# Seven common score banks, with the value sums of two units in any of them and added up by GpSimd

## The chip, the cores and the metric

The kernel uses one core of a Trainium2 chip. The metric is device time in microseconds, of one execution. TensorE (PE in the profile) multiplies and writes to PSUM, which has eight banks of 128 x 512 fp32; VectorE (DVE) and ScalarE (ACT) read PSUM; GpSimd (POOL) works on SBUF alone; the sync engine (SP) issues most DMAs.

## The reference

Two mixers of one input are gated and added. All is fp32; S = 2048 rows, D = 512 columns, 32 heads of 16.

```python
g = _sigmoid((x * gate_w).sum(-1, keepdims=True))
a = x @ dft_hid_re.T                     # hidden transform, real part
b = x @ dft_hid_im.T                     # and imaginary part
y_a = dft_seq_re @ a - dft_seq_im @ b    # 2048 x 2048 times 2048 x 512, twice
q, k, v = split(x @ wqkv)                # 32 heads of 16
p = softmax(q @ k.T * 16 ** -0.5)        # 2048 x 2048 for each head
y_b = concat(p @ v) @ wo
return g * y_a + (1 - g) * y_b
```

The softmax needs the maximum of each row of scores, or the exponentials overflow: the weights are scaled by 64.

## The kernel before

Products that need more than one fast fp32 pass are done in three: each operand is split into a high and a low part (`hi_lo`), and high x high, high x low and low x high are added in PSUM (`mm3`).

**Stages.** First q and k are made and stored, then v (into `vt`, 33 columns for each pair of heads: 16 of the even head, a column of ones, 16 of the odd head), then the imaginary hidden transform. Then comes the long middle part, which interleaves attention with the other work in three stages by one hand-written order: THIN (13 pairs of segments, beside the real hidden transform `real`), FULL (96 pairs, beside the sequence transform `dft`) and NINE (13 pairs, beside the output projection `proj`). An end part does the last pair of heads and what is left of the projection.

**Units.** Heads go in 16 pairs. The two heads of a pair lie in two halves of the partitions (`h` = 0, 1). For a pair and 1024 query columns, a unit `u` is one of 16 blocks of 128 keys: four score matmuls `s` (two blocks of 512 queries, two heads), each read by an exp on ACT into `pt` (four buffers), and then four value matmuls that take `pt` against 17 columns of `vt` (16 values and the ones, which give the sum of the row). The four go to four column groups of the array at the same time and add up over the 16 units in one PSUM bank, `acc`. After the 16th, ACT copies `acc` to `oe` and two DMAs store it.

**Maxima.** Well ahead of that, `a` tiles compute the same scores the other way round (128 queries by 512 keys), and DVE reduces each to its row maxima (`mx`). When all tiles of a pair and half are reduced, `m_parts` (DVE, then two small GpSimd operations) and, a segment later, `m_rows` (a DVE transpose, then four DMAs on SP's queue and four on GpSimd's) put the negative maxima as two extra rows under q, so that the score matmul subtracts them.

**A segment.** A pattern string is a segment; a letter is a slot. In each slot a matmul `d` of the interleaved work runs in one half of the rows (64 of 128), and a score, `a` or `s`, in the other half at the same time. Two letters in a slot are two scores and no `d`. `|` is the value matmuls of one unit, which use all rows. A pair of segments does the same `d`s with the one half of the rows and then with the other. The first `d` of a segment is given a wait by hand: for a reader of a score of the last slot of the segment before (`before`, `users`).

**Banks.** Scores `s` have a pool of three banks (`psS`), `a` tiles three (`psA`), `acc` one and `d` one (`psD`). A matmul into a bank waits until its last content has been read. Engines take their instructions in the order of the program.

**GpSimd** splits the chunks of the sequence matrix (`c_split`), three chunks ahead of their use, and does a few sums. LastPair handles the last pair of heads, whose units have other shapes.

Of the kernel before, what the change touches and what calls it, by code (L numbers as in the profile page):

```python
# [15 lines left out]
P = 128  # L16
# [15 lines left out]
def mix_kernel(ctx: ExitStack, tc: tile.TileContext, xa_t, xa, wqkv, w_hid, w_seq, wo, gate_w, out):  # L32
# [88 lines left out]

    banks = 0

    def bank():
        nonlocal banks
        banks += 1
        return (psS if banks % 2 else psA).tile([P, 512], F32, name="s" if banks % 2 else "a")


    with tc.tile_pool(name="qk", bufs=1, reuse_waits="tile") as pool:  # L130
# [26 lines left out]
        split(8)  # L157
        nc.vector.memset(acc, 0.0)

# [9 lines left out]
        for tb in range(4):  # L169
# [4 lines left out]
            for c in range(2):  # L174
                if tb == 0 and c == 0:
                    pss = [bank() for _ in range(4)]
                    for kt in range(KT):
                        for ct in range(4):
                            mm_qk(pss[ct], c, ct, tb, kt)
                    split(4)  # L180
                    for ct in range(4):
                        evac_qk(pss[ct], c, ct, tb)
                    continue
                for ct in range(4):
                    ps = bank()
# [28 lines left out]
    def a_tile(i, h, ps=None):  # L214
        p, j = divmod(i, 64)
        qt, kb = divmod(j, 4)
        if ps is None:
            ps = psA.tile([P, 512], F32, name="a")
        r = slice(64 * h, 64 * h + 48)
# [55 lines left out]
    for s in range(NT):  # L275
        t = xab[s // 4][:, s % 4]
        ps = psS.tile([P, 512], F32, name="s")
        for kt in range(KT):
# [20 lines left out]
    for s in range(NT):  # L299
        t = ab[s]  # L300
        ps = psS.tile([P, 512], F32, name="s")
        for kt in range(KT):
# [36 lines left out]


    class Chain:


        def __init__(self, pool, name, n):
            self.pool, self.name, self.left = pool, name, n
            self.begun = False

        def mm(self, st, mv, half, stop):
            if not self.begun:
                self.ps = self.pool.tile([P, 512], F32, name=self.name)  # L350
            r = slice(None) if half is None else slice(64 * half, 64 * half + 64)
# [4 lines left out]
    def real():  # L356

        for s, t in enumerate(ab):
            chain = Chain(psD, "d", 12)
            for kt in range(KT):  # L360
# [20 lines left out]
    def dft():  # L381

        for c in range(2):
            for tt in range(NT):
                chain = Chain(psD, "d", 48)
                yr = []
# [78 lines left out]
    def load_o(o, sm, hf, ct, q0, n=4):  # L465
# [69 lines left out]
    def proj(hf, cts, pools):  # L535

        for qt in range(8):
            t = hf * 8 + qt
            chain = Chain(*pools[qt % len(pools)], 3 * len(cts))
            for ct in cts:  # L540
# [32 lines left out]
    class LastPair:  # L573


        def __init__(self, blk, pools):
            self.blk, self.pools = blk, pools
            self.oe = work.tile([P, 512], F32, name="oe", bufs=2)
# [3 lines left out]

        def bank(self, i):
            pool, name = self.pools[i % len(self.pools)]
            return pool.tile([P, 512], F32, name=name)

        def copy(self, n):
            for c in range(n):
                cols = slice(c * 512 // n, (c + 1) * 512 // n)
                nc.scalar.copy(self.oe[:, cols], acc[:, cols])  # L590

        def turn(self):

            t = self.bank(0)
# [3 lines left out]
            nc.vector.reciprocal(self.rc, v[:, :, 16:48:16])  # L598
            for h in range(2):
                nc.vector.tensor_tensor(self.on[:, :, h], v[:, :, 33 * h:33 * h + DH],  # L600
                                        self.rc[:, :, h:h + 1].broadcast_to([P, 4, DH]), ALU.mult)

        def back(self):

            t = self.bank(1)
# [3 lines left out]
        def products(self, pools, others):  # L609

            pss = [pool.tile([P, 512], F32, name=name) for pool, name in pools]
            for i, (st, mv) in enumerate(((0, 0), (0, 1), (1, 0))):
# [11 lines left out]
    def last_pair(fill):  # L624
        few.append(work.tile([P, 4, D], F32, name="few", tag="pt", bufs=4))
        x = LastPair(1, [(psS, "s")])
        x.copy(4)
# [5 lines left out]
        drain(fill)  # L633
        x.products([(psA, "a"), (psA, "a"), (psS, "s"), (psS, "s")], (0,))

# [10 lines left out]

    def scores(u, qb, h, other=False):
        p, r = divmod(u, 32)
# [10 lines left out]
        nc.tensor.matmul(ps, ks[p % 2][rr, kt * P:(kt + 1) * P], qs[p % 2][rr, q0:q0 + 512], start=True, stop=True)  # L659
        return nc.scalar.activation(pts[u][:, 2 * qb + h], ps, AF.Exp, bias=0.0, scale=DH ** -0.5)  # L660

    def pv_last(u):
        blk, k2 = divmod(u - UNITS + 16, 8)
        pt = pts.pop(u)
        for j in range(4):
            x, h = divmod(j, 2)
            nc.tensor.matmul(acc[32 * j:32 * j + 17], vt[:, 2 * k2 + x, NP - 1, 16 * h:16 * h + 17], pt[:, j],  # L667
                             start=k2 == 0, stop=k2 == 7)
        if blk == 0 and k2 == 7:
            last_pairs.append(LastPair(0, [(psD, "d"), (psA, "a")]))  # L670
            last_pairs[0].copy(1)

    def pv(u):
        if u >= UNITS - 16:
            return pv_last(u)
        p, r = divmod(u, 32)
        hf, kt = divmod(r, 16)
        pt = pts.pop(u)
        for j in range(4):
            h = j % 2  # L680
            nc.tensor.matmul(acc[32 * j:32 * j + 17], vt[:, kt, p, 16 * h:16 * h + 17], pt[:, j],  # L681
                             start=kt == 0, stop=kt == NT - 1)
        if kt == NT - 1:
            oe = work.tile([P, 512], F32, name="oe", bufs=2)
            nc.scalar.copy(oe, acc)
# [15 lines left out]

    def issue(x, half, stop=True):
        chain, st, mv, after, last = x
        i = chain.mm(st, mv, half, last and stop)
# [29 lines left out]
    for p in range(1, NP):  # L734
        at(32 * (p - 1), load_stacks, p)
    one, more = [(psD, "d")], [(psD, "d"), (psA, "a"), (psA, "a")]
    at(456, load_yg, 0, range(3))
# [43 lines left out]
    def segment(pattern, half, ds, stop):  # L781


        nonlocal users
        before, users = users, []
        ds = iter(ds)
        for slot in pattern.split():
            if slot == "|":
                values()
                continue  # L790
            if len(slot) == 1:
                x = next(ds, None)
# [30 lines left out]
    for i in range(6):  # L823
# [5 lines left out]
        else:  # L829
            if i == 4:  # L830
                values()
                values()
            for _ in range(2):
# [18 lines left out]
    for u in range(valued + 2, UNITS, 2):  # L852
        run_plan(u)
        for i in range(4):
# [6 lines left out]
            for h in range(2):  # L861
                scores(u + i // 2, i % 2, h, h == 1)
        if u == 510:
            last_pairs[0].products([(psA, "a")] * 3 + [(psD, "d")], ())
        values()
        values()
    pv(UNITS - 2)
    pv(UNITS - 1)
    last_pair(last)


# [34 lines left out]
```

## Time and profile before

| | |
|---|---|
| time, three runs | 1738.14 us median (1738.07 to 1739.09) |
| span of the profiled execution | 1734.7 us |
| TensorE's granted clock | 0.998 |
| PE busy | 1717.7 us, 99% of the span |
| DVE, ACT, POOL busy | 1365.9, 1150.0, 442.6 us |
| reductions of `a` tiles (DVE) | 2026, 1244.9 us |
| exps (ACT) | 2008, 1024.3 us |
| value matmuls | 3968 and 128, each fp32 matmul in two passes |
| GpSimd's splits of chunks | 126 pairs, 77.1 and 162.2 us |

The page gives no time of the profiled execution beside its span; the three runs are other executions, and the median lies 3.4 us above the span. Times are counted from the first instruction. PE is the matmul, PEld the weight load. A row of the order of time gives the start, the duration, the engine, the line, the operation, out<-in and the count, and in brackets the engine's idle time before it with what ended it. A matmul's end is modelled, so that stalls are read from starts.

### The profile page before, as it was taken

The page shows a single profiled execution, that of the slowest core. Times are in us where ns is not written, and L with a number is a line of the kernel's source. Part 1 is how long each engine was busy: PE and PEld are TensorE (multiplying, and loading weights), DVE is VectorE, ACT ScalarE, POOL GpSimd, SP SyncE. Part 2 cuts the span into 40 slices and gives each one's busy share as a digit, 9 for nine tenths or more (in the row PEclk, how much of TensorE's full clock was granted, in tenths as well). Part 3 has the DMA queues.
Part 4 walks back from the last instruction along what each step waited for, and adds up shares of the span by engine and source line. Part 5 has one row for each costly group of instructions (what it writes and reads, how often), then busy time and mean ns, then how long its engine had stood idle before and what let it go on. Part 6 is the DMA issues. An engine that isn't in the chain of part 4 may idle for free.

```text
span 1734.7 us, 32901 instructions
## 1 busy us (share of the span) xinstructions
PE 1717.7 (99%) x12731; PEld 1037.9 (60%) x12731; DVE 1365.9 (79%) x2299; ACT 1150.0 (66%) x2255; POOL 442.6 (26%) x558
## 2 busy tenths in 40 slices
PE   8999999999999999999999999999999999999997
PEld 7876655556656666665666666566666666544443
DVE  5448688888888888888888888888888888899943
ACT  5211277777776777776677677767667777777775
POOL 0121122222222234222222343332233343200110
PEclk9999999999999999999999999999999999999999
DMA  9972500314141343314146535223142535560114
GB/s 293 334 156 109 158 3 8 56 31 80 39 92 44 75 106 88 76 41 78 40 92 238 100 105 106 73 60 71 44 86 63 124 99 92 177 152 15 38 28 134
DMA packets 82476, 165.05 MB, mean 95 GB/s; under 512 B 19776, under 2 KB 20032, under 8 KB 78480
## 3 DMA queue, kind: packets, MB, share of 16 engines
q1 hardware_dynamic: 77968, 162.56, 36.9%
q8 instruction: 100, 1.64, 0.4%
q0 software_dynamic: 4352, 0.39, 0.3%
q14 instruction: 56, 0.46, 0.1%
HBM read 107.73 MB, written 54.52 MB: 94 GB/s over the span
## 4 chain that ended last, share of the span: by engine, by line
PE 98%; DVE 1%; DMA 0%; issue 0%; ACT 0%; POOL 0%; DVEq 0%; SPq 0%; POOLq 0%; ACTq 0%
PE d L352 35%; PE acc L681 27%; PE a L220 13%; PE s L659 12%; PE s L82 3%; PE s L83 3%; PE s L84 3%; PE a L82 1%; PE a L84 1%; PE a L83 1%; PE acc L667 1%; DVE mx L222 0%; PE a L352 0%; DMA qs<-mt 0%; DMA raw<-xa_t 0%
## 5 line engine op out<-in xcount | busy, mean ns | idle before, releaser
L222 DVE TENSOR_REDUCE mx<-a 128x1 f32<-128x512 f32 x2026 | 1244.9, 682 | 252.7 <-PE a L220 235.1
L660 ACT ACTIVATE pt<-s 128x512 f32<-128x512 f32 x2008 | 1024.3, 622 | 390.3 <-PE s L659 326.5
L220 PE MATMUL a<-ks,qs 48*128 48x512 f32 x2026 | 811.8, 418 | 0.7 <-DVE mx L222 0.7
L659 PE MATMUL s<-qs,ks 50*128 50x512 f32 x2008 | 769.9, 413 | 1.1 <-DMA qs<-mt 0.7
L352 PE MATMUL d<-xab,ch 64*128 64x512 f32 x2016 | 648.4, 396 | 0.0
L681 PE MATMUL acc<-pt,vt 128*17 128x512 f32 x3968 | 485.6, 596 | 0.0
L352 PEld LDWEIGHTS d<-xab,ch 64*128 64x128 f32 x2016 | 366.0, 184 | 125.5 <-DVE mx L222 60.4
L659 PEld LDWEIGHTS s<-qs,ks 50*128 50x128 f32 x2008 | 366.2, 184 | 112.3 <-ACT pt L660 34.1
L220 PEld LDWEIGHTS a<-ks,qs 48*128 48x128 f32 x2026 | 366.1, 185 | 74.6 <-DVE mx L222 40.6
L352 PE MATMUL d<-xab,cl 64*128 64x512 f32 x1008 | 399.6, 396 | 0.0
L352 PEld LDWEIGHTS d<-xab,cl 64*128 64x128 f32 x1008 | 185.5, 184 | 64.9 <-DVE mx L222 40.8
L336 POOL CAST ch<-craw 128x512 fp32r<-128x512 f32 x126 | 77.1, 612 | 554.5 <-PE d L352 191.1
L681 PEld LDWEIGHTS acc<-pt,vt 128*17 128x17 f32 x3968 | 87.5, 96 | 198.2 <-issue 198.2
L337 POOL TENSOR_TENSOR cl<-craw,ch 128x512 fp32r<-128x512 f32 x126 | 162.2, 1287 | 10.2
L243 POOL DMA_DIRECT2D qs<-mt x128 | 72.0, 568 | 159.4 <-DVE mt L239 151.0
L352 PE MATMUL d<-wre,xab 64*128 64x512 f32 (+1 forms) x348 | 93.9, 402 | 0.0
L352 PEld LDWEIGHTS d<-wre,xab 64*128 64x128 f32 (+1 forms) x348 | 60.1, 185 | 31.8 <-issue 23.2
L352 PE MATMUL d<-wo_hl,o_hl 64*128 64x512 f32 (+1 forms) x261 | 71.1, 398 | 0.0
L78 ACT CAST hl<-s 128x512 fp32r<-128x512 f32 x32 | 18.7, 586 | 65.2 <-PE s L84 51.7
L352 PEld LDWEIGHTS d<-wo_hl,o_hl 64*128 64x128 f32 (+1 forms) x261 | 47.2, 185 | 16.0 <-issue 11.7
L234 POOL CAST nhl<-nm 128x16 fp32r<-128x16 f32 x32 | 6.3, 196 | 159.5 <-DVE nm L231 159.5
L369 POOL CAST xab<-y 128x512 fp32r<-128x512 f32 x16 | 9.8, 611 | 135.1 <-ACT y L368 107.2
(141 smaller groups left out, 944.2 us busy)
## 6 DMA issues: line engine op xcount, KB each, us to landing
craw<-w_seq SPq DMA_DIRECT2D x128, 256.0 KB
qk<-hl SPq DMA_DIRECT2D x32, 512.0 KB
qs<-qk SPq DMA_DIRECT2D x96, 128.0 KB
ks<-qk SPq DMA_DIRECT2D x96, 128.0 KB
b<-hl SPq DMA_DIRECT2D x16, 512.0 KB
xab<-b SPq DMA_DIRECT2D x16, 512.0 KB
o<-oe SPq DMA_DIRECT2D x62, 128.0 KB
oh<-nh SPq DMA_DIRECT2D x12, 512.0 KB
```

The source lines that it names most:

```text
L82: nc.tensor.matmul(ps, sh, mh, start=first, stop=False)
L83: nc.tensor.matmul(ps, sh, ml, start=False, stop=False)
L84: nc.tensor.matmul(ps, sl, mh, start=False, stop=last)
L220: nc.tensor.matmul(ps, qs[p % 2][r, qt * P:(qt + 1) * P], ks[p % 2][r, kb * 512:(kb + 1) * 512], start=True, stop=True)
L222: user = nc.vector.tensor_reduce(mx[p % 2][:, h, qt, kb:kb + 1], ps, AX.X, ALU.max)
L243: (nc.sync, nc.gpsimd)[h].dma_start(rows.rearrange("v (q b c) -> v b q c", q=8, b=4)[:, b], mt[hf][32 * b + h:32 * b + 32:2])
L336: nc.gpsimd.tensor_copy(h1, raw)
L337: nc.gpsimd.tensor_tensor(l1, raw, h1.bitcast(F32), ALU.subtract)
L352: i = nc.tensor.matmul(self.ps, st[r], mv[r], start=not self.begun, stop=stop)
L659: nc.tensor.matmul(ps, ks[p % 2][rr, kt * P:(kt + 1) * P], qs[p % 2][rr, q0:q0 + 512], start=True, stop=True)
L660: return nc.scalar.activation(pts[u][:, 2 * qb + h], ps, AF.Exp, bias=0.0, scale=DH ** -0.5)
L681: nc.tensor.matmul(acc[32 * j:32 * j + 17], vt[:, kt, p, 16 * h:16 * h + 17], pt[:, j], start=kt == 0, stop=kt == NT - 1)
```

## The change

- The three pools `psS`, `psA` and `psO` become seven pools of one bank. Before the middle part `turn_of` goes round them. In it, `bank` picks the bank that is expected to be free first, by an account that is kept in slots while the program is written: `now` goes on by one a slot and by 3.75 a value unit, a reader starts two slots after its matmul, a reduction takes 2.6 and an exp 2.1.
- Value sums: two units go together into whichever bank is picked (`values`, `pv`), eight matmuls in a row. ACT copies the bank out after each two units: the first two of a pair and half straight to `osum`, later ones to `oe`, which GpSimd then adds to `osum`. After the last two, `osum` is stored.
- A value matmul takes 32 columns of `vt` instead of 17, so that every row of the bank is written; the sum of the odd head lies in row 47 and its values in rows 48 to 63. The clearing of `acc` at the start is gone.
- The patterns: a segment has one value run of two units, at its end. FULL starts with `s` rather than `a`; THIN and NINE had two runs of one unit each.
- The last pair of heads holds one picked bank for each of its two blocks; the projection's chains at the end take picked banks too.

```diff
-    psS = ctx.enter_context(tc.tile_pool(name="psS", bufs=3, space=PSUM))
-    psA = ctx.enter_context(tc.tile_pool(name="psA", bufs=3, space=PSUM))
-    psO = ctx.enter_context(tc.tile_pool(name="psO", bufs=1, space=PSUM))
+    banks = [ctx.enter_context(tc.tile_pool(name=f"ps{i}", bufs=1, space=PSUM)) for i in range(7)]
...
-    acc = psO.tile([P, 512], F32, name="acc")
+    turns = dict.fromkeys("fsa", 0)
+
+    def turn_of(kind):
+        group = {"f": range(7), "s": range(3), "a": range(3, 7)}[kind]
+        turns[kind] += 1
+        return banks[group[(turns[kind] - 1) % len(group)]].tile([P, 512], F32, name="t")
...
-                a_tile(a_next, h, psD.tile([P, 512], F32, name="d") if j and h else None)
+                a_tile(a_next, h)
...
+    now, free, dve, act = 0.0, [0.0] * 7, 0.0, 0.0
+
+    def bank(i=None):
+        nonlocal now
+        if i is None:
+            i = min(range(7), key=lambda j: free[j])
+        now = max(now, free[i] + 0.7)
+        return i, banks[i].tile([P, 512], F32, name="t")
+
+    def read_by(i, kind):
+        nonlocal dve, act
+        if kind == "a":
+            dve = max(now + 2.0, dve) + 2.6
+            free[i] = dve + 0.4
+        else:
+            act = max(now + 2.0, act) + 2.1
+            free[i] = act + 0.5
...
-            s0 = 32 if h else 16
+            s0 = 47 if h else 16
...
-            o0 = 33 if h else 0
+            o0 = 48 if h else 0
...
-    def scores(u, qb, h, other=False):
+    def scores(u, qb, h):
...
-        ps = psA.tile([P, 512], F32, name="a") if other else psS.tile([P, 512], F32, name="s")
+        i, ps = bank()
+        read_by(i, "s")
...
-    def pv(u):
-        if u >= UNITS - 16:
-            return pv_last(u)
-        p, r = divmod(u, 32)
-        hf, kt = divmod(r, 16)
-        pt = pts.pop(u)
-        for j in range(4):
-            h = j % 2
-            nc.tensor.matmul(acc[32 * j:32 * j + 17], vt[:, kt, p, 16 * h:16 * h + 17], pt[:, j],
-                             start=kt == 0, stop=kt == NT - 1)
+    osum = work.tile([P, 2, 512], F32, name="osum", tag="w15")
+
+    def pv(us):
+        nonlocal now
+        i, acc = bank()
+        for u in us:
+            p, r = divmod(u, 32)
+            hf, kt = divmod(r, 16)
+            pt = pts.pop(u)
+            for j in range(4):
+                h = j % 2
+                nc.tensor.matmul(acc[32 * j:32 * j + 32], vt[:, kt, p, h:h + 32], pt[:, j],
+                                 start=u == us[0], stop=u == us[-1])
+        now += 3.75 * len(us) + 1
+        read_by(i, "s")
+        o = osum[:, hf]
+        if kt + 1 == len(us):
+            nc.scalar.copy(o, acc)
+            return
+        oe = work.tile([P, 512], F32, name="oe", bufs=2)
+        nc.scalar.copy(oe, acc)
+        nc.gpsimd.tensor_tensor(o, o, oe, ALU.add)
         if kt == NT - 1:
-            oe = work.tile([P, 512], F32, name="oe", bufs=2)
-            nc.scalar.copy(oe, acc)
             for qb in range(2):
-                nc.sync.dma_start(o_d[hf][p, :, qb * 512:(qb + 1) * 512], oe[64 * qb:64 * qb + 64])
+                nc.sync.dma_start(o_d[hf][p, :, qb * 512:(qb + 1) * 512], o[64 * qb:64 * qb + 64])
...
-    FULL = "a s a s a s s a s a s a s a s a | |"
-    THIN = "aS s s a a s a | a s a a s s sA |"
-    NINE = "sA s s a a sA | a a s a s aS |", "aS a s s a aS | sA a s a s s sA |"
+    FULL = "s a s s a a s s a a s a s a s a |"
+    THIN = "sA a s a s a s s a s a s a aS |"
+    NINE = "sA s s a a sA a a s a s aS |", "aS a s s a aS sA a s a s s sA |"
...
     def score(kind, h):
         x = next(streams[h][kind == "a"], None)
         if x:
-            users.append((kind, (a_tile if kind == "a" else scores)(*x)))
+            if kind == "a":
+                i, ps = bank()
+                read_by(i, "a")
+                users.append((kind, a_tile(*x, ps)))
+            else:
+                users.append((kind, scores(*x)))
 
     def values():
         nonlocal valued
-        pv(valued)
-        valued += 1
+        us = valued, valued + 1
+        valued += 2
+        if us[0] < UNITS - 16:
+            pv(us)
+        else:
+            for u in us:
+                pv_last(u)
```

More of the change, by code (lines that the diff above doesn't have):

```diff
@@ L175, in mix_kernel @@
                 if tb == 0 and c == 0:
-                    pss = [bank() for _ in range(4)]
+                    pss = [turn_of("f") for _ in range(4)]
                     for kt in range(KT):
@@ L338, in c_split, with d_bank, o_bank, __init__ @@
             hls[i] = (h1, l1)
+    def d_bank():
+        return psD.tile([P, 512], F32, name="d")
+    now, free, dve, act = 0.0, [0.0] * 7, 0.0, 0.0
[13 more added lines that the diff above has]
+            free[i] = act + 0.5
+    def o_bank(kind="a"):
+        i, t = bank()
+        read_by(i, kind)
+        return t
     class Chain:
-        def __init__(self, pool, name, n):
-            self.pool, self.name, self.left = pool, name, n
+        def __init__(self, take, n):
+            self.take, self.left = take, n
             self.begun = False
@@ L358, in real @@
         for s, t in enumerate(ab):
-            chain = Chain(psD, "d", 12)
+            chain = Chain(d_bank, 12)
             for kt in range(KT):
@@ L384, in dft @@
             for tt in range(NT):
-                chain = Chain(psD, "d", 48)
+                chain = Chain(d_bank, 48)
                 yr = []
@@ L589, in copy @@
                 cols = slice(c * 512 // n, (c + 1) * 512 // n)
-                nc.scalar.copy(self.oe[:, cols], acc[:, cols])
+                nc.scalar.copy(self.oe[:, cols], self.acc[:, cols])
         def turn(self):
-            t = self.bank(0)
+            t = o_bank()
             for c in range(4):
@@ new lines, in mix_kernel @@
+    osum = work.tile([P, 2, 512], F32, name="osum", tag="w15")
+    def pv(us):
+        nonlocal now
+        i, acc = bank()
+        for u in us:
[15 more added lines that the diff above has]
+        nc.gpsimd.tensor_tensor(o, o, oe, ALU.add)
@@ L702, in issue @@
     def issue(x, half, stop=True):
+        nonlocal now
+        now += half is None
         chain, st, mv, after, last = x
@@ L735, in mix_kernel @@
         at(32 * (p - 1), load_stacks, p)
-    one, more = [(psD, "d")], [(psD, "d"), (psA, "a"), (psA, "a")]
+    one, more = [d_bank], [d_bank, o_bank, o_bank]
     at(456, load_yg, 0, range(3))
@@ L790, in segment @@
                 continue
+            now += 1
             if len(slot) == 1:
```

60 lines of the change are left out of this document (28 added, 32 removed).

## The prediction

> **What bounds the kernel now.** I read the page first, for the totals and the chain of waits; then the busy time by windows, to part the stages; then the order of time of one segment (one pass of a pattern string), engine by engine.
>
> ```profile
> span 1734.7 us, 32901 instructions
> PE 1717.7 (99%) x12731; PEld 1037.9 (60%) x12731; DVE 1365.9 (79%) x2299; ACT 1150.0 (66%) x2255; POOL 442.6 (26%) x558
> PE 98%; DVE 1%; DMA 0%; issue 0%; ACT 0%; POOL 0%; DVEq 0%; SPq 0%; POOLq 0%; ACTq 0%
> L222 DVE TENSOR_REDUCE mx<-a 128x1 f32<-128x512 f32 x2026 | 1244.9, 682 | 252.7 <-PE a L220 235.1
> ```
>
> PE carries 98% of the chain, but its busy time contains stalls of a few tenths that show only in the order of time. The stages that the change touches:
>
> ```profile
> 220.00:370.00 150.00, 150.00 (x1125) 75.18 (x1121) 130.07 (x211) 113.42 (x219) 34.35 (x47) 1.00 0.15 24
> 1520.00:1636.00 116.00, 115.89 (x840) 54.05 (x832) 109.06 (x180) 85.81 (x167) 9.81 (x20) 1.00 0.24 56
> 600.00:700.00 100.00, 100.00 (x809) 61.40 (x808) 82.64 (x140) 72.16 (x144) 36.37 (x42) 1.00 0.47 101
> 700.00:800.00 100.00, 100.00 (x810) 61.84 (x806) 82.85 (x140) 71.08 (x141) 26.13 (x34) 1.00 0.33 66
> 375.73 1.91 PE L681 MATMUL acc<-pt,vt 128*17 128x512 f32 x16
> 1513.44 1.91 PE L681 MATMUL acc<-pt,vt 128*17 128x512 f32 x16
> ```
>
> After the window's own length come PE, PEld, DVE, ACT and POOL busy. The first row is the THIN stage, the second NINE, the next two FULL. In FULL nobody is at 100% but PE. The last two rows are the first and the last of the 192 value runs of FULL: 1137.7 us over 191 gaps, 5.96 us a segment (5.95 in the one below). FULL is two thirds of the time, so its segment decides. One of them, PE first, then DVE and ACT:
>
> ```profile
> 806.07 0.50 PE L352 MATMUL d<-xab,ch 64*128 64x512 f32 x1
> 806.08 0.50 PE L220 MATMUL a<-ks,qs 48*128 48x512 f32 x1
> 806.41 0.40 PE L659 MATMUL s<-qs,ks 50*128 50x512 f32 x1
> 809.59 0.40 PE L659 MATMUL s<-qs,ks 50*128 50x512 f32 x1
> 809.64 0.39 PE L352 MATMUL d<-xab,ch 64*128 64x512 f32 x1
> 809.83 0.42 PE L220 MATMUL a<-ks,qs 48*128 48x512 f32 x1
> 810.18 1.91 PE L681 MATMUL acc<-pt,vt 128*17 128x512 f32 x16
> 812.02 0.50 PE L352 MATMUL d<-xab,ch 64*128 64x512 f32 x1
> 806.62 4.88 DVE L222 TENSOR_REDUCE mx<-a 128x1 f32<-128x512 f32 x8 [1.08 <-PE a L220]
> 806.88 4.03 ACT L660 ACTIVATE pt<-s 128x512 f32<-128x512 f32 x8 [1.98 <-PE s L659]
> ```
>
> Take the first `d` as 0. The second slot starts at 0.34, the sixteenth `d` at 3.57, so a slot takes 0.23. The scores fall behind the `d`s: the last `a` starts at 3.76. Its bank is that of the third `a` before it, the fifth reduction's. DVE starts 0.54 after the first `a` and takes 8 in 4.88; with 0.68 for one alone (L222's mean) that is one each 0.60, so the fifth ends at 0.55 + 4 x 0.60 + 0.68 = 3.63, and the `a` follows 0.13 later. So three maximum banks set the last slot. From there: 0.35 to the value run, 1.84 to the next `d`: 5.95. The same sum without a bank wait: last slot at 3.56, value run at 3.92, next segment at 5.76. That is what the change can get at most in FULL: 0.19 a segment.
>
> **The change part by part.** *Seven common banks.* From the built program, a steady FULL segment after the change (s a s s a a s s a a s a s a s a) takes banks 5 2 4 3 1 0 6 5 2 4 1 3 0 6 5 2 and bank 1 for the run; each is one last read by a known exp or reduction. To walk it I need the new copy on ACT and the delay from a score to its reader:
>
> ```profile
> 542.41 1.91 PE L681 MATMUL acc<-pt,vt 128*17 128x512 f32 x16
> 544.25 0.50 PE L352 MATMUL d<-xab,cl 64*128 64x512 f32 x1
> 544.39 0.59 ACT L685 COPY oe<-acc 128x512 f32<-128x512 f32 x1 [1.26 <-PE acc L681]
> 301.92 0.40 PE L220 MATMUL a<-ks,qs 48*128 48x512 f32 x1
> 302.36 0.69 DVE L222 TENSOR_REDUCE mx<-a 128x1 f32<-128x512 f32 x1 [0.26 <-PE a L220]
> ```
>
> A copy starts 0.14 after the next segment's first `d`; an exp follows it after about 0.49 (the eight above: (4.03 - 0.62) / 7). So exps start at 0.62 + 0.49k and bank 5, read by the fifth (slot 7), is free at 2.58 + 0.61 + 0.13 = 3.32; slot 14 wants it at 3.33. Reductions: the first `a` is now in slot 1 (0.34), not slot 0, and an `a` outside a segment's first slot is read 0.44 after it starts: 0.78. The second `a` is in slot 4 (1.03): its reduction starts at 1.47, not 1.38, a hole of 0.09; from there one each 0.60. Bank 0 (third reduction) is free at 2.07 + 0.68 + 0.13 = 2.88, wanted at 2.87. So no bank costs more than 0.02, and slots and run keep the 5.76.
>
> *What is late next.* `segment` makes its first `d` wait for a user of the score issued in the last slot of the segment before; in FULL that is the last `a`, its eighth reduction. Before, it ended at 0.55 + 7 x 0.60 + 0.68 = 5.43, half a microsecond early. After, with the first `a` 0.23 later and the hole, it ends at 1.47 + 6 x 0.60 + 0.68 = 5.75; with 0.13 for the signal the next `d` cannot start before 5.87 to 5.88. A segment behind the end of a chain (every sixth, 32 of 192) has no such wait. So 160 segments fall from 5.95 to 5.87 (12.8 us) and 32 from 5.95 to 5.76 (6.1): FULL gives 19. Bounds: 37 when that wait counts for nothing, 10 when reductions and signals run 0.06 longer.
>
> *Copies and sums.* 217 new copies and 31 as before on ACT, 217 new adds on POOL. Their nearest rows, and the groups that bear on the other stages:
>
> ```profile
> L352 PEld LDWEIGHTS d<-xab,ch 64*128 64x128 f32 x2016 | 366.0, 184 | 125.5 <-DVE mx L222 60.4
> L681 PEld LDWEIGHTS acc<-pt,vt 128*17 128x17 f32 x3968 | 87.5, 96 | 198.2 <-issue 198.2
> L685 ACT COPY oe<-acc 128x512 f32<-128x512 f32 x31 | 18.2, 587 | 31.9 <-PE acc L681 31.8
> L410 POOL TENSOR_TENSOR y<-y,yr 128x512 f32<-128x512 f32 x16 | 20.4, 1277 | 53.5 <-ACT y L409 53.2
> 299.96 0.58 ACT L368 COPY y<-d 128x512 f32<-128x512 f32 x1
> 300.43 3.09 ACT L660 ACTIVATE pt<-s 128x512 f32<-128x512 f32 x6
> 220.50 1.13 PE L681 MATMUL acc<-pt,vt 128*17 128x512 f32 x8
> 370.61 1.05 PE L681 MATMUL acc<-pt,vt 128*17 128x512 f32 x8
> 305.89 1.05 PE L681 MATMUL acc<-pt,vt 128*17 128x512 f32 x8
> 306.87 0.50 PE L220 MATMUL a<-ks,qs 48*128 48x512 f32 x1
> ```
>
> 217 x 0.587 = 127 us go into ACT's idle time (1.98 before the eight exps above); 217 x 1.277 = 277 us into POOL, which goes from 26% to about 42%. Two `oe` buffers let an add be two segments late. Both cost nothing while that cover holds; the rivals price its loss. Value weights of 32 columns in place of 17: a load of 17 takes 0.096 and one of 128 takes 0.184, so one of 32 should take some 0.01 more; only a run's first load shows, 2 us in all at most, and I take 0.
>
> *THIN, NINE.* 26 segments each; one value run of two units instead of two runs. A run of one takes 0.98 from its start to the next slot, a run of two 1.84; with a second entry (0.35 instead of a slot's 0.23) and a second long first slot (0.34) a split costs about 0.35. The Trainium skill's page TensorEngine Tiling (Array Packing), section Key Properties, says that a change of tiling mode drains TensorE; by that rule alone the 52 merged segments would give 52 x 0.35 = 18 us more. The rows speak against counting it. THIN: DVE is at 130.07 of 150, and the second unit of every other segment needs the exp of the very last score, behind 7 exps and the `y` copy (0.47 to the next exp): 0.62 + 7 x 0.49 + 0.47 + 0.61 + 0.13 = 5.26, then a second pass 0.43 and the way out 0.52: 6.21. Its neighbour has no `y`: 14 slots to 3.10, 0.36, 1.84, 5.30 without bank waits, 5.6 with 0.3 of them (16 scores in 14 slots outrun both readers). The mean, 5.75 to 5.9, stands against 5.89 now (25.5 segments between the runs that start at 220.50 and 370.61). I take 0; bounds 6 gained, 6 lost. NINE: DVE is busy 109.06 of 116 and keeps its work; I take 0, bounds 4 each way. Start and end stages keep their work and order; the end has 3 of the copies. 0, bounds 3 each way.
>
> *Sum.* -19 us on a span of 1734.7. The runs shown have a median of 1738.14, 3.4 above that span, which I carry over: 1719. Own range of this case 1709 to 1730.
>
> **The rivals.** (1) *The last reduction's wait does not bind*: data arrive earlier, or the hole closes. For it: it lies only 0.11 above the 5.76. Against: it is a sum of measured steps. FULL at 5.76: 1738 - 37 = 1701. (2) *Merging pays in THIN and NINE as the drain rule has it*: 1719 - 18 = 1701; against it stands the exp of the last score. (3) *Slower: ACT.* The copy now heads ACT's queue in every segment and all eight exps queue behind it, bank 5's among them, which has 0.01 to spare. If the copy starts x later than 0.14, slot 14, the run and the segment move by x: 5.76 + x. Below x = 0.11 the other wait hides it, at x = 0.19 the gain is gone. At x = 0.32 (the start that `read_by` itself assumes, two slots after the run) FULL is at 6.08, +25, and THIN follows with about 26 x 0.2 = 5: 1768; at 0.25, 1750. For: margins are thin. Against: 0.14 is measured, and ACT is idle then. (4) *POOL is late with the maxima rows.*
>
> ```profile
> 817.88 2.24 POOL L243 DMA_DIRECT2D qs<-mt  x4 [5.70 <-DVE mt L239]
> qs<-mt POOLq DMA_DIRECT2D x128, 2.0 KB, 1.7
> 825.95 0.41 PE L659 MATMUL s<-qs,ks 50*128 50x512 f32 x1
> ```
>
> The four issues of `m_rows` now queue behind an add: copy 0.14 + 0.59, add 1.28, so from about 2.1 after the segment's start instead of 0; 2.24 of issue and 1.7 to land: 6.0. The first score that reads them is in the segment after, slot 7: 5.87 + 1.7 = 7.6. Spare 1.5 (4.1 now: 825.95 - 820.12 - 1.7). A split of a chunk (1.9) between add and issues makes it 0.4 late: 30 x 0.4 = 12, 1731. (5) *It does nothing*: the scores' lag is PE's own and not the banks': 1738. Against: the lag starts only when the fourth reuse comes. (6) *GpSimd blocks DVE.* The two FULL windows above have POOL at 36.37 and 26.13 and DVE at 82.64 and 82.85 for 140 operations each: no trace of it. If an add held up the reductions by its length, FULL would be at about 7.1, 1960. The Trainium skill's Perfetto Trace Analysis, section Optimizing Scalar/DVE Operations, warns that GpSimd and DVE share an SBUF read port; the trace does not bear that out for these reductions, which read PSUM.
>
> **How the numbers follow.** Forecast 0.45; (1) 0.13; (2) 0.05; (3) 0.15; (4) 0.08; (5) 0.10; (6) 0.02; 0.02 for what I don't see. 0.2% is 3.5 us, about what a measurement of this kernel tells from no change. Below 1734.7: the forecast, (1), (2), most of (4), a little of (5): 0.73. Within: most of (5): 0.08. Above: (3), (6) and the rest: 0.19. The range 1700 to 1742 takes in all but (3), (6) and the unseen.
>
> **What would show it.** FULL runs 5.87 apart, 5.76 behind a chain's end; last score 3.56 after the first `d`, the first `d` waiting for DVE; DVE's hole of 0.09 behind each segment's first reduction; copies 0.14 behind the first `d`; THIN in turns of about 5.5 and 6.2. Runs at 5.95 or more, or copies later than 0.3, would make it wrong.

## The result and the profile after

The changed kernel takes 1728.47 us (median; 1727.76 to 1731.44), the kernel before on the same chip 1738.41 (1738.07 to 1739.09). The ratio is 0.9948, 95% interval 0.9934 to 0.9962: faster by 9.9 us, where 19 had been predicted. The profiled execution of the changed kernel is the slowest of its four, so its span, 1729.6, lies only 5.1 below the 1734.7 of before.

The page's head, its chain, and the groups of the reductions, scores, adds and copies:

```profile
span 1729.6 us, 33828 instructions
PE 1707.6 (99%) x12731; PEld 1083.8 (63%) x12731; DVE 1375.7 (80%) x2298; ACT 1250.4 (72%) x2472; POOL 715.1 (41%) x775
PE 96%; DMA 1%; POOL 1%; DVE 1%; issue 1%; ACT 0%; SPq 0%; DVEq 0%; POOLq 0%; ACTq 0%
L219 DVE TENSOR_REDUCE mx<-t 128x1 f32<-128x512 f32 x2048 | 1268.1, 682 | 233.8 <-PE t L217 203.5
L682 PE MATMUL t<-qs,ks 50*128 50x512 f32 x2048 | 750.8, 416 | 7.6 <-DMA qs<-mt 5.7
L728 POOL TENSOR_TENSOR osum<-osum,oe 128x512 f32<-128x512 f32 x217 | 280.4, 1292 | 671.2 <-ACT oe L727 662.6
L727 ACT COPY oe<-t 128x512 f32<-128x512 f32 x217 | 127.5, 587 | 260.6 <-PE t L718 258.8
```

The sizes of the new work are as forecast (copies 127 us, adds 280, GpSimd at 41%, reductions still 682 ns). What is new is that 7.6 us of idle time stand before the scores, 5.7 of it for the maxima rows (`qs<-mt`), where the kernel before had 1.1 and 0.7, and that TensorE holds 96% of the chain instead of 98%.

The same segment as the eye follows it, TensorE first, then VectorE and ScalarE:

```profile
746.82 1.93 PE L718 MATMUL t<-pt,vt 128*32 128x512 f32 x16
748.68 0.49 PE L378 MATMUL d<-xab,cl 64*128 64x512 f32 x1
752.23 0.39 PE L378 MATMUL d<-xab,cl 64*128 64x512 f32 x1
752.31 0.40 PE L217 MATMUL t<-ks,qs 48*128 48x512 f32 x1
752.63 1.92 PE L718 MATMUL t<-pt,vt 128*32 128x512 f32 x16
754.50 0.49 PE L378 MATMUL d<-xab,cl 64*128 64x512 f32 x1
749.48 4.96 DVE L219 TENSOR_REDUCE mx<-t 128x1 f32<-128x512 f32 x8 [0.86 <-PE t L217]
748.87 0.59 ACT L727 COPY oe<-t 128x512 f32<-128x512 f32 x1 [1.32 <-PE t L718]
749.35 4.03 ACT L683 ACTIVATE pt<-t 128x512 f32<-128x512 f32 x8
```

Run to run is 5.81; the kernel before stood at 5.95 in practically every segment. The last score starts 3.63 behind the first `d` (before: 3.76) and 0.08 behind the `d` of its own slot, so the bank wait of the last slot is gone. Three of four segments of FULL lie at 5.80 to 5.84: over 191 gaps 5.957 - 5.817 = 0.14 each, some 27 us, more than the 19 forecast. But the mean over these gaps is 5.912, so about 18 of the 27 are given back, by segments like these:

```profile
604.76 1.93 PE L718 MATMUL t<-pt,vt 128*32 128x512 f32 x16
611.06 1.93 PE L718 MATMUL t<-pt,vt 128*32 128x512 f32 x16
729.21 1.92 PE L718 MATMUL t<-pt,vt 128*32 128x512 f32 x16
735.17 1.93 PE L718 MATMUL t<-pt,vt 128*32 128x512 f32 x16
1487.98 2.80 PE L718 MATMUL t<-pt,vt 128*32 128x512 f32 x16
1494.66 1.92 PE L718 MATMUL t<-pt,vt 128*32 128x512 f32 x16
```

Of the first kind (6.30) there are 12, each 0.49 over the usual: 6 us. Of the second (5.96), 16, each 0.16: 2.5. Single ones: 12.34 up to the run at 1487.98 and 6.68 behind it, 7.4 over; 7.67 up to 917.87, 1.85 over. With some 0.4 of small ones that is 18. What stands in each of the first three kinds, in the order of time (ScalarE at the first; TensorE's weight loads at the second, with a usual one under it) and in the waits of TensorE (the changed kernel, then the kernel before):

```profile
606.80 0.59 ACT L727 COPY oe<-t 128x512 f32<-128x512 f32 x1 [1.30 <-PE t L718]
607.29 0.62 ACT L83 CAST nh<-no 128x512 fp32r<-128x512 f32 x1
607.81 4.02 ACT L683 ACTIVATE pt<-t 128x512 f32<-128x512 f32 x8
731.07 0.18 PEld L378 LDWEIGHTS d<-xab,ch 64*128 64x128 f32 x1 [0.85 <-DVE mx L219]
731.25 0.18 PEld L682 LDWEIGHTS t<-qs,ks 50*128 50x128 f32 x1
742.86 0.18 PEld L378 LDWEIGHTS d<-xab,ch 64*128 64x128 f32 x1 [0.85 <-DVE mx L219]
742.86 0.18 PEld L682 LDWEIGHTS t<-qs,ks 50*128 50x128 f32 x1
```

```profile
PE t L682 <- DMA qs<-mt: 5.7, 2, 4.3
PE s L659 <- DMA qs<-mt: 0.7, 1, 0.7
```

At 607.29 the cast of the normalised block (`block`, step 2) stands between the new copy and the first exp; all eight exps are 0.5 later than behind a copy alone (1.01 behind the copy's start instead of 0.48). At 731.25 the first score's weights load 0.18 behind the `d`'s instead of together with them: it is the first score of a new half pair, which in the built program waits for four transfers at once. The last two rows say that the maxima rows came late twice in the whole run, 5.7 us together, and that in the kernel before they had come late once already, by 0.7 near 1493: its one uneven segment in FULL, of 6.95, is there.

### The profile page after: what moved, and what is told of

The parts are those of the page before. It is cut to its first block, busy times and chain, and to the rows that moved or that the text cites. A ratio compares the mean times of both kernels' runs of the same rounds, so it can differ in the third digit from the quotient of the medians.

```text
span 1729.6 us, 33828 instructions
## 1 busy us (share of the span) xinstructions
PE 1707.6 (99%) x12731; PEld 1083.8 (63%) x12731; DVE 1375.7 (80%) x2298; ACT 1250.4 (72%) x2472; POOL 715.1 (41%) x775
## 4 chain that ended last, share of the span: by engine, by line
PE 96%; DMA 1%; POOL 1%; DVE 1%; issue 1%; ACT 0%; SPq 0%; DVEq 0%; POOLq 0%; ACTq 0%
PE d L378 36%; PE t L718 27%; PE t L217 11%; PE t L682 11%; PE t L87 4%; PE t L88 3%; PE t L89 3%; PE t L699 1%; DMA qs<-mt 1%; POOL osum L728 0%; DVE mx L219 0%; PE t L378 0%; DMA raw<-xa_t 0%; DVE yp L559 0%; POOL qs L240 0%
## 5 line engine op out<-in xcount | busy, mean ns | idle before, releaser
L219 DVE TENSOR_REDUCE mx<-t 128x1 f32<-128x512 f32 x2048 | 1268.1, 682 | 233.8 <-PE t L217 203.5
L683 ACT ACTIVATE pt<-t 128x512 f32<-128x512 f32 x2048 | 1038.9, 633 | 19.4 <-PE t L682 12.0
L682 PE MATMUL t<-qs,ks 50*128 50x512 f32 x2048 | 750.8, 416 | 7.6 <-DMA qs<-mt 5.7
L217 PE MATMUL t<-ks,qs 48*128 48x512 f32 x2048 | 711.7, 402 | 0.1
L728 POOL TENSOR_TENSOR osum<-osum,oe 128x512 f32<-128x512 f32 x217 | 280.4, 1292 | 671.2 <-ACT oe L727 662.6
L718 PE MATMUL t<-pt,vt 128*32 128x512 f32 x3968 | 486.5, 599 | 0.0
L682 PEld LDWEIGHTS t<-qs,ks 50*128 50x128 f32 x2048 | 367.0, 185 | 83.1 <-ACT pt L683 23.6
L217 PEld LDWEIGHTS t<-ks,qs 48*128 48x128 f32 x2048 | 362.7, 186 | 45.1 <-DVE mx L219 19.7
L727 ACT COPY oe<-t 128x512 f32<-128x512 f32 x217 | 127.5, 587 | 260.6 <-PE t L718 258.8
L718 PEld LDWEIGHTS t<-pt,vt 128*32 128x32 f32 x3968 | 105.3, 109 | 238.1 <-issue 156.2
```

Of the source, the lines that this page charges most:

```text
L217: nc.tensor.matmul(ps, qs[p % 2][r, qt * P:(qt + 1) * P], ks[p % 2][r, kb * 512:(kb + 1) * 512], start=True, stop=True)
L219: user = nc.vector.tensor_reduce(mx[p % 2][:, h, qt, kb:kb + 1], ps, AX.X, ALU.max)
L718: nc.tensor.matmul(acc[32 * j:32 * j + 32], vt[:, kt, p, h:h + 32], pt[:, j], start=u == us[0], stop=u == us[-1])
L728: nc.gpsimd.tensor_tensor(o, o, oe, ALU.add)
```

## The experiments

Ratios are to the kernel before on the same chip, with 95% intervals; the changed kernel's is 0.9948. Differences in microseconds between two runs carry up to 1 us more, since the kernel before took 1737.40 to 1738.41 us beside them.

**The cast off ScalarE.** In `block`, step 2:

```diff
-            hi_lo(hl[:, 0], hl[:, 1], t[:, 0], nc.gpsimd)
+            nc.gpsimd.tensor_copy(hl[:, 0], t[:, 0])
+            nc.gpsimd.tensor_tensor(hl[:, 1], t[:, 0], hl[:, 0].bitcast(F32), ALU.subtract)
```

> The changed kernel with the cast of the normalised block (12 of them, 0.62 us each) on GpSimd instead of ScalarE. My theory: in the changed kernel this cast stands right behind the value copy at the head of ScalarE's queue, so that all eight exps of 12 segments are 0.5 late; without it these 12 segments fall from 6.31 to 5.82, 6 us, total 1722.5 (0.991 of the kernel before). The block's tail on GpSimd gets 1.3 us longer per block; if that is late somewhere it eats 1 to 3 of it. Rival: the 12 segments are long because of the block's other work (loads on SP, the subtraction on GpSimd); then they stay at 6.3 and the total at 1728.5 (0.995).

1722.80 us, 0.9914 (0.9899 to 0.9929): 5.7 less than the changed kernel. No segment is left near 6.3; where the cast had been, the exps follow the copy at once:

```profile
606.90 0.59 ACT L728 COPY oe<-t 128x512 f32<-128x512 f32 x1 [1.32 <-PE t L719]
607.38 4.03 ACT L684 ACTIVATE pt<-t 128x512 f32<-128x512 f32 x8
```

The late rows near 915 and 1480 stay (segments of 7.34 and 11.93). So the cast behind the copy cost what was counted for it.

**The maxima steps ahead of the value run.** In `segment`:

```diff
             if slot == "|":
+                if deferred:
+                    deferred.pop(0)()
                 values()
                 continue
...
-        if deferred:
-            deferred.pop(0)()
```

> The changed kernel with the deferred maxima steps issued before a segment's value run instead of behind it, so that GpSimd's four transfers of maxima rows stand ahead of the add and not behind it. My theory: the add puts these issues 2.1 us later in GpSimd's queue, and at the two places where the transfer takes over 5 us (near 910 and 1477 us, beside bulk loads) TensorE waits; with the issues 1.5 to 2 us earlier the wait at 915 (1.9) goes and that at 1483 (4.3, with 3 us of slower matmuls behind it) is halved at least: 4 to 8 us less, total 1721 to 1725. Rival: the waits come from the bulk loads and from a gap inside GpSimd's issuing, not from the add: 0 to 1 us, total 1728, with the waits in their places.

1724.41 us, 0.9922 (0.9908 to 0.9937): 4.1 less. The wait near 915 is gone, the later one halved, and the two segments that had taken 12.34 and 6.68 take 8.43 and the usual 5.8:

```profile
PE t L682 <- DMA qs<-mt: 2.2, 1, 2.2
```

The place in GpSimd's queue is thus one cause of the late rows; what is left of the wait needs another (see the last experiment). This edit issues the transfers earlier as well as ahead of the add; that it is the add that holds them back, few adds shows.

**Both.**

> Both edits together: the block's cast on GpSimd and the maxima steps ahead of the value run. My theory: the two costs are independent, so the gains add: 10 to 14 us below the changed kernel, total 1715 to 1719, which is the predicted 1719. Rival: the longer block tail on GpSimd makes the maxima rows late again: no better than the better of the two, 1722 or more.

1717.94 us, 0.9890 (0.9873 to 0.9907): 10.5 less than the changed kernel, 1.1 from the predicted 1719. Apart from 22 segments of 5.96 to 6.01 hardly one is out of line before 1470, and one of 8.48 is left there. The two costs add up.

**Few adds.**

```diff
-        nc.gpsimd.tensor_tensor(o, o, oe, ALU.add)
         if kt == NT - 1:
+            nc.gpsimd.tensor_tensor(o, o, oe, ALU.add)
```

> The changed kernel without 186 of the 217 adds on GpSimd: of each eight value sums of a half pair only the first and the last are added up, so the values of the output are left out in part. If the adds cost time (GpSimd's queue, or an SBUF port shared with VectorE), it falls: by my theory by what the late maxima rows cost where an add stands ahead of them, 2 to 9 us (1719 to 1726), with reductions still 0.598 apart. Rival, a shared port: reductions closer than 0.598 and segments shorter all through, 20 us or more. Rival, the adds cost nothing at all: 1728.

1722.69 us, 0.9912 (0.9897 to 0.9928): 5.8 less. This kernel leaves out most of the sum. The wait near 915 is gone, the cast's segments stay, and near 1480 the wait is down to 2.3 us, so only 2.0 of the 4.3 there were the adds'; yet segments of 10.38 and 6.99 remain there: the clock fell behind it (last section). Eight reductions of an undisturbed segment take the same time with and without adds (without, then the changed kernel):

```profile
748.69 4.95 DVE L219 TENSOR_REDUCE mx<-t 128x1 f32<-128x512 f32 x8 [0.85 <-PE t L217]
755.29 4.95 DVE L219 TENSOR_REDUCE mx<-t 128x1 f32<-128x512 f32 x8 [0.85 <-PE t L217]
```

The adds cost where they stand ahead of the maxima rows, and nothing on VectorE.

**Six common banks, the sum held in the seventh.** The value runs of 16 units add up in one bank, as before; scores and maxima share six:

```diff
-            i = min(range(7), key=lambda j: free[j])
+            i = min(range(6), key=lambda j: free[j])
...
-        i, acc = bank()
+            if kt == 0:
+                sums_now[:] = [banks[6].tile([P, 512], F32, name="t")]
+            acc = sums_now[0]
...
-                                 start=u == us[0], stop=u == us[-1])
+                                 start=kt == 0, stop=kt == NT - 1)
```

> The changed kernel with its value sums held in one bank over 16 units as in the kernel before, and the six other banks common to scores and maxima: none of the 217 new copies on ScalarE and none of the 217 adds on GpSimd; order and merged value runs as in the changed kernel. My theory: the gain of the large stage comes from the common banks alone, and what is given back (casts behind the copies, 6 us; maxima rows behind the adds, 9 us) comes from the copies and adds. Then the usual segment stays at 5.80 to 5.85, the segments at 6.31 are gone, the waits near 915 and 1483 us fall to what the kernel before had: total 1712 to 1717. Rival: the seventh bank is needed, six don't do: segments of 5.90 or more, total 1728 or more.

1746.96 us, 1.0048 (1.0035 to 1.0060): my theory fell, the rival held. Nearly all segments are back at 5.91 to 6.01. One of them, the eight exps and the last two scores:

```profile
702.67 0.49 PE L378 MATMUL d<-xab,ch 64*128 64x512 f32 x1
703.21 4.04 ACT L683 ACTIVATE pt<-t 128x512 f32<-128x512 f32 x8 [1.89 <-PE t L682]
706.16 0.42 PE L682 MATMUL t<-qs,ks 50*128 50x512 f32 x1
706.42 0.40 PE L217 MATMUL t<-ks,qs 48*128 48x512 f32 x1
```

By the program's own choice of banks the last `a` here takes the bank of the sixth exp: 703.21 + 5 x 0.48 + 0.64 + 0.13 = 706.38, and it starts at 706.42, 3.75 behind the first `d`: the old place. But for the one copy at the end of a sum there are no copies and no adds, and there is no segment of 6.3. The maxima rows still come 1.7 us late near 1496 (a segment of 9.41), so that wait needs no add. So one pool for both kinds is not enough; with this order it is the seventh bank, which only summing up in SBUF sets free, that pays.

**The same with two value runs in THIN and NINE** (the patterns of before, `|` for one unit, `||` for two).

> The kernel with six common banks and a held sum, and in the thin and nine stages the old patterns with two value runs of one unit a segment, in place of one run of two. My theory: merging costs in the nine stage (turns of 5.725 on average against 5.56 for two runs before, 23 segments, 4 us) and does nothing in the thin one: 3 to 5 us below the kernel with merged runs, 1708 to 1713. Rival, the drain rule (each split of a run costs about 0.35 for 52 segments): 18 us above it. Rival: no difference, the nine stage lost by the copies.

1738.54 us, 1.0011 (1.0002 to 1.0019): 8.4 less than with merged runs, and no better than the kernel before. The 5.56 in that expectation was a misreading; the two runs of before come to 5.71 over 46 units. When the runs are split, THIN's turns fall from 6.01 to 5.94 per two units and NINE's from 5.88 to 5.73. With six banks merging costs, in THIN too, where no difference had been expected.

**The old order of FULL under seven banks.**

```diff
-    FULL = "s a s s a a s s a a s a s a s a |"
+    FULL = "a s a s a s s a s a s a s a s a |"
```

> The changed kernel with the old order of the sixteen scores in the large stage (a s a s a s s a s a s a s a s a) in place of the new one, all else as changed. My theory: seven banks in one pool pay whatever the order, the new order only keeps the casts and copies off a bank that is wanted soon: usual segments 5.80 to 5.88, total 1724 to 1735. Rival: the order is what pays, since two maxima early put VectorE ahead: usual segments at 5.95, total 1738 or more once the casts and late rows are added.

1720.58 us, 0.9894 (0.9879 to 0.9909): better than the new order by 7.9, which neither view had expected. Usual segments take 5.79, the cast's segments 6.08 instead of 6.31, and segments of 5.96 don't occur. A run, the `d` behind it, and the eight reductions between the run before and this `d`:

```profile
725.79 1.92 PE L718 MATMUL t<-pt,vt 128*32 128x512 f32 x16
727.64 0.49 PE L378 MATMUL d<-xab,ch 64*128 64x512 f32 x1
722.39 4.88 DVE L219 TENSOR_REDUCE mx<-t 128x1 f32<-128x512 f32 x8 [0.89 <-PE t L217]
```

With that, 12 x 0.23 (casts), 16 x 0.16 and some 150 x 0.03 make about 10, where 7.9 were measured.

**Only the first two scores swapped.**

```diff
-    FULL = "s a s s a a s s a a s a s a s a |"
+    FULL = "a s s s a a s s a a s a s a s a |"
```

> The changed kernel with the first two scores of the large stage's order swapped (a s s s a a s s ... in place of s a s s a a s s ...), nothing else. My theory: what the old order gains over the new one (1720.6 against 1728.5) lies in its first slot: a score that begins a new half pair waits for several transfers with two semaphore instructions of 51 ns each, and as the first slot it holds up the row of slots behind the first d (23 segments of 5.97 in place of 5.82, 3.6 us); behind an a it doesn't, and the reductions begin 0.23 earlier. So the 5.97 segments are gone and the total is 1722 to 1726. Rival: the gain lies in the alternation further back, which lets the casts and copies cost less: the 5.97 segments may go, but the cast's segments stay at 6.3 and the rest at 5.82 or above, total 1726 or more.

1744.88 us, 1.0040 (1.0026 to 1.0054): slower by 16 than the changed kernel; my theory fell, and the rival's "1726 or more" holds but is far too low. The usual segment is 5.93:

```profile
729.71 0.59 ACT L727 COPY oe<-t 128x512 f32<-128x512 f32 x1 [0.72 <-PE t L718]
730.30 4.03 ACT L683 ACTIVATE pt<-t 128x512 f32<-128x512 f32 x8
732.94 0.46 PE L682 MATMUL t<-qs,ks 50*128 50x512 f32 x1
733.24 0.40 PE L217 MATMUL t<-ks,qs 48*128 48x512 f32 x1
```

With an `a` in front the first exp starts 0.59 behind the copy's start instead of 0.48. Slot 14 takes the bank of the fifth exp, as in the new order: 730.30 + 4 x 0.48 + 0.65 + 0.13 = 733.00. Its score starts at 732.94 and takes 0.46 instead of the usual 0.39, and the score behind it starts 3.72 after the segment's first `d` (at 729.52) instead of 3.63: these 0.09 are most of what the segment lost. The prediction's walk had given this bank 0.01 to spare. In the old order slot 14 takes the bank of the fourth reduction, 0.2 after it is free, and the fifth exp's bank is wanted only in slot 15, 0.13 after it is free, so a late exp costs less. The order's worth lies in which reader frees the bank of the last slots, not in its first slot.

**Old order, cast and maxima steps moved**: the three edits together.

> Seven common banks with the old order in the large stage, the block's cast on GpSimd, and the maxima steps ahead of the value run. My theory: the three costs are independent: from 1720.6, 3.4 off for the casts (12 x 0.28) and 4 to 7 off for the late rows (7.24 and 12.46 + 6.57 shrink as they did): 1710 to 1714. Rival: the old order hides one of them already or brings a new wait: 1716 or more.

1707.19 us, 0.9824 (0.9810 to 0.9837): the best, 21.3 less than the changed kernel and 30.9 less than the one before (1738.07 beside it); the 1710 to 1714 that had been expected were too cautious. Nearly all of FULL lies at 5.78 to 5.82:

```profile
span 1705.4 us, 33828 instructions
PE t L683 <- DMA qs<-mt: 1.1, 1, 1.1
```

**Runs split again**, on top of that: in NINE, and in NINE and THIN, two runs of one unit into one bank that is held in between.

> As the kernel with old order, cast and rows moved, and in the nine stage the old patterns: two value runs of one unit a segment, both into the one bank that is held from the first to the second, so that copies and adds are as many as before. My theory: merging costs 3 to 5 us there (turns of 5.725 on average against 5.56 before): total 3 to 5 below that kernel. Rival: the bank held over both runs is the one that is missed, as with six banks: turns of 5.75 or more, 0 to 6 above it. Rival, the drain rule: 23 splits of 0.35, 8 above it.

> As the one before, with two runs of one unit in the thin stage too. My theory: turns of 5.9 on average either way: no difference, within 2 us. Rival, the drain rule: 26 splits of 0.35, 9 above the kernel with merged runs in the thin stage. Rival: the second unit of a merged run waits for the last exp (turns of 6.21), which a split avoids: 4 to 8 below.

1710.28 us, 0.9841 (0.9827 to 0.9855), and 1715.15 us, 0.9870 (0.9856 to 0.9884). In NINE two units take 5.75 split and 5.72 merged, and what follows FULL is 1.0 longer when split. The totals differ by 3.1, the profiled executions by 5.1, of which 3.2 lie in the wait for maxima rows: it comes before NINE and was longer there (2.8 us, with segments of 10.02 and 6.33, instead of 1.1, with 7.36). With the same NINE and THIN split too it was 0.9, with 7.10; why it varies is open. In THIN a split costs: 6.13 against 5.89, some 24 x 0.24 = 6, and 4.9 between the totals. My views of both stages fell; merging is worth about 1 us in NINE and 5 in THIN.

**The bulk loads later**, on top of the best kernel: the loads of the output weights and normalised blocks are issued four chunks later (the weights at 1471.1 in the profiled execution instead of 1458.5).

```diff
-            end_tiles(s // 4)
+            if s > 3:
+                end_tiles(s // 4 - 1)
+            if s == NT - 1:
+                end_tiles(3)
```

> As the kernel with old order, cast and rows moved (1707.2), and the bulk loads of the output weights and the normalised blocks at the end of the large stage issued four chunks (1.5 segments) later each, the last two together. My theory: the last wait for maxima rows (the segment of 7.36 there, of 12.46 with 6.57 behind it where the rows stand behind the add) has two causes: the place in GpSimd's queue, and the bulk loads that are issued a microsecond before the fourth of GpSimd's transfers, which then takes 4.7 to 6.8 us to land in place of 1.7. With the loads later no segment there is over 5.9: 1.6 less, total 1704 to 1707. Rival: the late landing is not the loads' doing; the segment stays over 7, total 1707, or more if the nine stage then waits for its weights.

1714.40 us, 0.9862 (0.9846 to 0.9879): 7.2 more than the kernel that it is built on, where 0 to 3 less had been expected. The maxima rows near the end of FULL now land in 1.7 us, all of them, and nobody waits for them; but the first projections of NINE wait for the loads instead. The landing of these rows in the changed kernel, in the kernel that this one is built on, and here, and then TensorE's longest wait here:

```profile
DMA to landing us min/median/max: 1.7/2.6/6.3
DMA to landing us min/median/max: 1.7/1.7/4.7
DMA to landing us min/median/max: 1.7/1.7/1.7
```

```profile
PE d L378 <- DMA o_hl<-oh: 5.6, 1, 5.6
```

So the bulk loads are the other half of the late rows near 1480; near 915 this was not tried. The Trainium skill's page Trainium Kernel Development and Optimization, section Key Constraints, says that transfers issued from SP and from GpSimd run on the same 16 DMA engines and interleave; these rows agree.

## Why the prediction was right or wrong

**Direction, mechanism and the banks: right.** The last slot's wait for the bank of the third maximum before it set FULL's pace, and seven common banks took it away. The walk was right to a tenth, its thin margins too: shifting the exps by 0.1 (first two swapped) undid the gain, and six banks brought the wait back.

**FULL's usual segment: gain too small by about 8 us.** Forecast 5.87, with the next `d` held by the eighth reduction; measured 5.81 to 5.82. The step that gave too little is the 0.13 for the signal behind the eighth reduction. The reductions themselves end where the prediction has them, 5.76 behind the first `d` (5.75 forecast), but the wait for them hardly binds: in the changed kernel they end at 749.48 + 4.96 = 754.44 and the `d` starts at 754.50, 0.06 later and 1.87 behind the run; in the old order they end 0.37 before the `d`, and it stands 1.85 behind the run all the same. Rival (1) was right on the wait. Its 5.76 was not reached, since the last score starts at 3.63, not 3.56.

**The failed step: "Both cost nothing while that cover holds".** Copies and adds were taken at 0, and what lost its cover was not their own work but their neighbours'. The copy took the 1.98 us in front of the exps in which ScalarE's cast had been free: 12 x 0.49, and 5.7 measured by moving it. This is rival (3)'s mechanism, segments of 5.76 + x, but with x = 0.5 in 12 segments rather than a little in all; the prediction had priced the copy alone, which started 0.19 behind the first `d`, not 0.14. The adds made the maxima rows late as rival (4) said, but in 2 half pairs out of some 30, at the two places where bulk transfers stretch the landing from 1.7 to 5.5 and 6.3. The late rows cost 9 there in the profiled execution (a slower clock included); moving them ahead of the adds gave 4.1 in the median, leaving the adds out 5.8. The rest is the bulk loads': the prediction's spare of 1.5 us counted a landing of 1.7, read at an undisturbed place. Together the term taken at 0 measured 10.5: with cast and rows moved, the changed kernel stands at 1717.94. That this is 1.1 from the predicted 1719 is partly luck: 8 us of gain that was not forecast stand against 22 x 0.17 for the first scores of half pairs and 2.7 for the late rows that are left. In the profiled execution FULL came to 27 - 18 = 9 (1129.3 us over the 191 gaps instead of 1137.7) instead of 19.

**Not foreseen: the first score of a half pair** waits for several transfers, and in front of a segment it costs 0.16. In the kernel before, such a delay, the casts and the late rows near 915 vanished in the bank wait: its segments were even because the bank wait was the longest in nearly all. Only the late row near 1493 showed. That the others vanished there is read from the even 5.95; it wasn't tried by itself.

**THIN and NINE: right.** THIN's mean turn is 5.89 as before, with turns of 5.57 and 6.22 as worked out; NINE takes 5.73 per two units against 5.71, and what follows FULL is 2.1 longer in all, inside the bounds. By the drain rule of rival (2), merging should have paid in every stage; it pays 5 us in THIN and about 1 in NINE with seven banks, and costs with six. So the free banks weigh more than the change of tile, whose own price these runs don't part from the waits for banks. **(6)** is out: reductions take 682 ns with GpSimd at 26% and at 41%. **(5)** is out as well, since the bank wait is gone.

## What to carry to other kernels

A wait that recurs in every turn hides all smaller ones; before taking it away, list what happens in its shadow only now and then (a cast, a transfer beside bulk loads, an instruction with many waits), and price each for the turns in which it falls, since that can be half of the gain, as it was here. Work put into another engine's idle time cost nothing itself here, but it cost by what queued behind it, so look at what stood there. When banks are shared, an order of work is good if the late slots take banks whose readers are long done; shifting one reader by 0.1 us cost 16 us here.

## What the hardware showed that was not expected

A stop of TensorE can cost twice. The granted clock is the third column from the end. In the changed kernel, behind its wait of 4.3 us:

```profile
1483.70:1487.00 3.30, 3.13 (x15) 2.70 (x17) 1.90 (x3) 1.33 (x3) 0.00 (x0) 0.50 0.03 5
1487.00:1490.00 3.00, 3.00 (x17) 0.90 (x17) 1.45 (x3) 1.06 (x2) 0.00 (x0) 0.53 0.00 0
1490.00:1494.00 4.00, 4.00 (x36) 3.07 (x29) 2.49 (x4) 3.09 (x7) 1.29 (x1) 1.00 0.00 0
```

With few adds, behind a wait of 2.3 us at 1476.9 (from 1483 to 1486 the clock is still at 0.54):

```profile
1480.00:1483.00 3.00, 3.00 (x15) 2.25 (x13) 2.41 (x4) 1.80 (x4) 0.00 (x0) 0.50 0.08 27
```

With six banks, behind a wait of 1.7 us:

```profile
1498.00:1501.00 3.00, 3.00 (x17) 2.47 (x13) 2.32 (x4) 1.79 (x3) 0.00 (x0) 0.51 0.27 102
1501.40:1505.00 3.60, 3.60 (x33) 1.92 (x33) 1.64 (x3) 1.88 (x5) 0.00 (x0) 0.99 0.00 0
```

With cast and maxima steps moved, behind a wait that is 2.3 us again:

```profile
1474.00:1478.00 4.00, 3.49 (x29) 2.23 (x33) 2.75 (x5) 2.22 (x4) 0.01 (x1) 1.00 0.33 124
```

Behind the first two the clock is at half for some 6 us (a value run takes 2.80 instead of 1.92), which costs about 3; behind the third for some 3 us. A wait of 2.3 us once brought it and once didn't, and one of 1.7 did, so the length of the wait alone doesn't decide; what else does is open. The Trainium skill's page TensorE: Matmul & The Clock Gate, section HAM oscillation, warns of idle gaps above about 3.4 us; here a shorter one was enough, so the measurement goes against the figure.
